# Hash-bucketed attention on one core: queries and keys turned in token order by VectorE, with contiguous casts, hashes and signs, and moves for two pairs at once

## The chip, the cores and the metric

The kernel runs on one core of one Trainium2 chip. The metric is the device time of one execution in microseconds; a kernel's time is the median of its runs. Besides these runs there is one profiled execution of each kernel, from which all rows below come.

## What is computed

Attention over 4 batches of 8 heads, 768 tokens of 64 dimensions each. A query sees only the keys with the same six hash bits. Its output goes through a mixture of eight low-rank adapters, of which each token uses the two with the largest gates.

```python
q_bits = (np.einsum('bhsd,dk->bhsk', q, proj) > 0)          # six bits per token
k_bits = (np.einsum('bhsd,dk->bhsk', k, proj) > 0)
mask   = q_bucket[:, :, :, None] == k_bucket[:, :, None, :]  # buckets: the bits as a number
scores = np.where(mask, q @ k.T / sqrt(64), -1e9)
attn   = softmax(scores)
x      = attn @ v                                            # as (3072, 512)
out    = x + sum over the two chosen e of w_e * (x @ A[e]) @ B[e]
```

## The kernel before, in words

**Pairs and tiles.** The 32 heads are worked on as 16 pairs of heads, p = 0 to 15; a batch has four pairs. For the first 14 pairs the scores of a pair are 9 tiles of 128 x 1024, stored keys by queries; the last two pairs are cut into groups of token blocks, so that the end can be worked off early. For each tile TensorE multiplies (`sc`), ScalarE takes the exponential into the buffer P (`ex`, L344), and TensorE multiplies with the values (`pv`, L366) into the one PSUM bank V, of which column 64 of each block is the softmax's sum. VectorE takes the reciprocal and multiplies (`rec`, `norm`), POOL casts the result (`xcast`), TensorE turns it (`xturn`), and per batch the adapters follow (`lzm`, `top`, `dif`, `sel`, `gexp`, `gate`, `zmul`, `delta`, `addx`, `store`).

**The mask as a part of the product.** The operands of the score matmul live in a tile aug: rows 0 to 63 are q or k of one head, transposed, and the rows from 64 on hold the hash bits as signs. For pairs 1 to 15 these are six rows and a constant one, 71 in all. Equal buckets add a constant to the score, and each differing bit takes enough away that the exponential is nothing. Where a query finds no key the softmax has to be uniform: for that, V begins with a tiny multiple (2 to the -56) of the sum of the values. POOL sums the values (`vsum`, L319 to L323), TensorE spreads the sum over the partitions (`uni`, L326, into the bank n), VectorE copies it out (`ucopy`, L330) and then into V ahead of each group (`seed`, L355 and L358).

**How a pair's aug is made.** Each partition holds six neighbouring tokens of a head (`l`, L272), so loads run over 1536 bytes. VectorE transposes 32 x 32 blocks of q or of k of both heads in one instruction of 768 elements (`t`, L278); in R the blocks lie by token within the partition, so the columns aren't in token order. POOL casts R to bf16 and puts the columns in order with the same instruction (`c`, L281): it writes 2-byte elements in steps of 12 bytes. SP then moves quarter-rows into aug, 8 DMAs a pair (`mv`, L286). Beside that TensorE hashes R in fp32 (`h`, L295), reading columns in steps of 256 bytes into n; VectorE turns the result into signs (`sn`, L299) and scales them (`sm2`, L303), and SP writes them to DRAM and back into the sign rows (`sdw`, `sdr`, L307 and L310). aug, P and R have four, three and two buffers.

**The first pair** is made faster: its tokens are transposed by TensorE, VectorE and ScalarE copy them out, POOL casts them into aug (`ca`, L250), TensorE hashes them (`ha`, L258), and VectorE writes 18 sign rows straight from PSUM (`sa`, L265), again in steps of 12 bytes; its aug has 82 rows.

**Order.** Each engine works its instructions in the order of a long string of such names (ORDER), written out by hand or by a planner; a name `mv.4.2.1` is the method with its arguments, mostly the pair first. SP's queue carries nearly all DMAs. An instruction that waits holds up all that stand behind it on its engine.

Of the kernel before, what the change touches and what calls it, by code (L numbers as in the profile page):

```python
# [75 lines left out]
class Kernel:  # L76

    def __init__(self, ctx, tc, q, k, v, proj, w_gate, A, Bm, out):
# [48 lines left out]
        self.ssc = t("ssc", [1])
        self.iq = t("iq", [4])
        self.thr = t("thr", [1])
        self.mul = t("mul", [1])  # L130
# [16 lines left out]
    def const2(self):  # L147
        nc = self.nc
        row = self.ident.rearrange("p (c r) -> p c r", c=4)
        iq, red = self.iq, nc.vector.tensor_reduce  # L150
        red(out=iq[:, 0:1], in_=row[:, 0:2, 12:18], axis=AX.XY, op=ALU.add)
        red(out=iq[:, 1:2], in_=row[:, 2:4, 6:12], axis=AX.XY, op=ALU.add)
        nc.vector.tensor_tensor(out=iq[:, 2:3], in0=iq[:, 0:1], in1=iq[:, 1:2], op=ALU.add)
        nc.vector.tensor_scalar(out=self.thr, in0=iq[:, 2:3], scalar1=-1.0, scalar2=None, op0=ALU.mult)
        nc.vector.tensor_scalar(out=self.mul, in0=iq[:, 2:3], scalar1=-48.0, scalar2=32.0,
                                op0=ALU.mult, op1=ALU.add)

    def const3(self):
        nc = self.nc
        row = self.ident.rearrange("p (j b i) -> p j b i", j=4, b=8)  # L160
        iq = self.iq
        nc.vector.memset(self.ssc, 32.0)
        for k, s in enumerate((-34.0, 3040.0)):
            nc.vector.tensor_reduce(out=iq[:, k:k + 1], in_=row[:, k::2, 6, :], axis=AX.XY, op=ALU.add)
# [536 lines left out]
```

## Time and profile before

| | |
|---|---|
| median of 3 runs | 240.85 us (237.78 to 241.51) |
| the profiled execution's own time | 237.42 us |
| its span | 235.6 us |
| mean granted clock of TensorE | 0.878 |
| busy: TensorE, VectorE, ScalarE, POOL | 184.8, 159.1, 147.6, 162.4 us |
| first exponential starts, last one ends | 17.98 us, 224.05 us |
| DMA: bytes, packets, share of the 16 engines (queue q1) | 32.67 MB, 41,021, 47.8% |

In the profile's rows a group is a line of the kernel on one engine: L281 is line 281, "POOL CAST Rb<-R 128x768" the engine, the operation, what it writes from what, and partitions x elements; after the count come busy time, the mean of one in ns, and the idle time of the engine just before, with what ended most of it. PE is TensorE's matmuls, PEld its weight loads, DVE is VectorE, ACT ScalarE, SPq the issuing of DMAs by SP. Matmuls are pipelined, so a busy PE isn't PE at its peak. The granted clock is the share of TensorE's clock that the throttle let through.

### The profile page before, as it was taken

What the parts mean: (1) busy time and instruction counts of PE and PEld (TensorE: products, weight loads), DVE (VectorE), ACT (ScalarE), POOL (GpSimd) and SP (SyncE); (2) the same over time, 40 slices, a digit from 0 to 9 for tenths busy, and PEclk for the clock granted to TensorE, in tenths of its full rate; (3) what the DMA queues carried; (4) which work ended last, traced back from release to release, by engine and by line L of the source; (5) the groups of instructions that cost most, each with busy time, mean ns of one, the idle gap of its engine ahead of it and who ended that gap; (6) DMA issues with size and microseconds to landing.
All of it is one profiled execution on the core that took longest, in us unless ns stands there. A gap on an engine that the chain in (4) does not pass through costs nothing.

```text
span 235.6 us, 5542 instructions
## 1 busy us (share of the span) xinstructions
PE 184.8 (78%) x2131; PEld 114.1 (48%) x2131; DVE 159.1 (68%) x364; ACT 147.6 (63%) x163; POOL 162.4 (69%) x168
## 2 busy tenths in 40 slices
PE   6566398598869999499867899979499965989652
PEld 2212143256346675275643556846255543877420
DVE  2799966369263479459857758986357963666894
ACT  2106188468755998377866868969467744799310
POOL 3899999996799698499757979892349990231000
PEclk9656589889985999679999999999769977899995
DMA  6911742684786661694366615564722322300445
GB/s 216 336 50 28 192 132 52 178 229 134 181 223 137 164 184 45 190 276 133 95 179 212 183 34 160 145 207 147 203 69 82 85 50 67 123 3 3 187 162 188
DMA packets 41495, 33.36 MB, mean 142 GB/s; under 512 B 25433, under 2 KB 38397, under 8 KB 41469
## 3 DMA queue, kind: packets, MB, share of 16 engines
q1 hardware_dynamic: 41021, 32.67, 47.8%
q8 instruction: 17, 0.28, 0.5%
q10 hardware_dynamic: 448, 0.33, 0.4%
q14 instruction: 9, 0.07, 0.1%
HBM read 20.06 MB, written 7.03 MB: 115 GB/s over the span
## 4 chain that ended last, share of the span: by engine, by line
PE 25%; POOL 24%; DVE 18%; DMA 9%; SPq 9%; issue 9%; ACT 4%; ACTq 0%; DVEq 0%; POOLq 0%
POOL Rb L281 17%; PE s L339 10%; SPq L286 7%; PE v L366 6%; DVE aug L265 6%; ACT P L344 4%; DMA aug<-Rb 4%; PE n L295 3%; DVE acc L490 3%; POOL va L319 3%; DMA proj<-in_proj_dram 2%; DMA vn<-in_v_dram 2%; DVE R L278 2%; DMA aug<-dr 2%; POOL vs L323 1%
## 5 line engine op out<-in xcount | busy, mean ns | idle before, releaser
L344 ACT ACTIVATE P<-s 128x1024 bf16<-128x1024 f32 (+1 forms) x146 | 142.9, 1045 | 64.2 <-PE s L339 62.1
L339 PE MATMUL s<-aug 71*128 71x256 bf16 (+4 forms) x432 | 101.5, 337 | 16.3 <-DMA aug<-Rb 9.1
L281 POOL CAST Rb<-R 128x768 bf16<-128x768 f32 x30 | 88.5, 3032 | 11.5 <-DMA aug<-Rb 10.4
L339 PEld LDWEIGHTS <-aug 71*128 71x128 bf16 (+1 forms) x432 | 45.3, 130 | 59.1 <-issue 36.7
L366 PEld LDWEIGHTS <-P 128*128 128x128 bf16 x1152 | 53.7, 103 | 22.1 <-issue 13.5
L366 PE MATMUL v<-vb,P 128*128 128x65 bf16 x1152 | 58.4, 200 | 3.4 <-DVE v L355 2.0
L295 PE MATMUL n<-R,hst 128*32 128x192 f32 x240 | 33.1, 610 | 1.9 <-POOL Rb L281 1.3
L278 DVE STREAM_TRANSPOSE R<-nat 128x768 f32<-128x768 f32 x30 | 29.8, 997 | 4.1 <-POOL Rb L281 3.9
L401 POOL CAST xb<-x 128x768 bf16<-128x768 f32 (+1 forms) x18 | 13.6, 756 | 27.3 <-DVE x L382 20.3
L319 POOL TENSOR_TENSOR va<-vn 128x384 f32<-128x384 f32 x16 | 17.7, 1116 | 6.2 <-DMA vn<-in_v_dram 6.1
L490 DVE SCALAR_TENSOR_TENSOR acc<-n,rt,x 128x512 f32<-128x512 f32 x17 | 12.7, 749 | 12.6 <-PE n L486 12.1
L382 DVE TENSOR_TENSOR x<-v,ri 128x384 f32<-128x384 f32 x28 | 16.8, 600 | 0.7
L299 DVE TENSOR_SCALAR sg<-n 128x192 bf16<-128x192 f32 x15 | 5.2, 349 | 17.4 <-PE n L295 17.4
L355 DVE COPY v<-u 128x390 f32<-128x390 f32 x28 | 15.8, 564 | 0.6
L314 POOL CAST vb<-vn 128x768 bf16<-128x768 f32 x16 | 13.5, 850 | 0.7 <-PE v L366 0.7
L413 DVE COPY xT<-n 128x768 bf16<-128x768 bf16 (+1 forms) x18 | 8.7, 484 | 7.1 <-PE n L408 6.8
L250 POOL CAST aug<-R 64x128 bf16<-64x128 f32 (+2 forms) x14 | 12.3, 1010 | 0.7 <-ACT R L243 0.5
L295 PEld LDWEIGHTS n<-R,hst 128*32 128x32 f32 x240 | 7.0, 120 | 11.8 <-issue 3.5
L303 DVE TENSOR_SCALAR s<-sg,ssc 128x192 bf16<-128x192 bf16 x15 | 12.5, 833 | 0.2
L372 DVE RECIPROCAL ri<-v 128x6 f32<-128x6 f32 x28 | 6.3, 225 | 9.0 <-PE v L366 8.6
L408 PE MATMUL n<-ident_bf,xb 128*128 128x128 bf16 x92 | 8.4, 225 | 2.5 <-DVE rt L466 2.3
L326 PE MATMUL n<-vs,eps 128*128 128x130 bf16 x16 | 3.8, 238 | 7.6 <-POOL vs L323 7.0
(83 smaller groups left out, 158.7 us busy)
## 6 DMA issues: line engine op xcount, KB each, us to landing
vn<-in_v_dram SPq DMA_DIRECT2D x16, 384.0 KB
nat<-in_k_dram SPq DMA_DIRECT2D x15, 384.0 KB
...
aug<-Rb SPq DMA_DIRECT2D x120, 48.0 KB
...
dr<-s SPq DMA_DIRECT2D x15, 48.0 KB
...
nat<-in_q_dram SPq DMA_DIRECT2D x2, 192.0 KB
```

The source lines that it names most:

```text
L265: self.nc.vector.tensor_scalar(out=self.augt(slice(64, 82), h, i, e, u, n), in0=self.hb(h)[r, u * P:(u + n) * P].rearrange("d (u p) -> d u ...
L278: self.nc.vector.transpose(out=self.R[p % 2][:, i], in_=self.nat[p % 3][:, i])
L281: self.nc.gpsimd.tensor_copy(out=self.Rb[p % 2][:, :, i].rearrange("p h f (c t) -> p h t f c", t=T), in_=self.R[p % 2][:, i].rearrange("p ...
L286: (self.nc.sync, self.nc.gpsimd)[eng].dma_start(out=self.aug[p % 4][32 * f:32 * f + 32, :, 192 * a:192 * a + 192], in_=self.Rb[p % 2][32 * ...
L295: self.nc.tensor.matmul(out=hs[32 * j:32 * j + 32], lhsT=self.hst[:, f].rearrange("p b i -> p (b i)"), rhs=rhs, start=(f == 0), stop=(f == ...
L319: add(out=a, in0=vn[:, :, 0:3, :], in1=vn[:, :, 3:6, :])
L339: self.nc.tensor.matmul(out=self.Sb[n % 3][:, o:o + qw], lhsT=aug[rows, 2 * h + 1, kt::T], rhs=aug[rows, 2 * h, q0:q0 + qw], start=True, s ...
L344: self.nc.scalar.activation(out=self.Pt[p % 3][:, at:at + w], in_=self.Sb[n % 3][:, 0:w], func=ACT.Exp, scale=0.125)
L355: self.nc.vector.tensor_copy(out=self.pvv(p, g), in_=self.u[p % 2][:, g:g + 1, :].to_broadcast([P, T, D + 1]))
L366: self.nc.tensor.matmul(out=v[:, i, :], lhsT=self.Pt[p % 3][:, o:o + P], rhs=self.vb[p % 3][:, h, kt, :], start=False, stop=(kt == T - 1), ...
L382: self.nc.vector.tensor_tensor(out=x[:, :, c:c + D], in0=v[:, :, 0:D], in1=self.ri[g % 2].unsqueeze(2).to_broadcast([P, T, D]), op=ALU.mult)
L490: self.nc.vector.scalar_tensor_tensor(out=self.acc[(m // 2) % 3][:, m % 2, lo:hi], in0=self.bank(bank)[:, lo:hi], scalar=self.rt[g % 2][:, ...
```

## The change

- **Transposes** (`t`): one instruction per head, 384 elements, reading q or k as before and writing R in token order, halves of the head dimension apart: the output steps 24 bytes from element to element.
- **Casts and hashes** (`c`, `h`): both now read R, and the cast writes Rb, in runs.
- **Signs**: the projection is negated once (`projx`). The signs are made by two bitwise operations on the upper half of each fp32 hash in PSUM (`bits`): sign bit kept, magnitude 16. That replaces compare, subtract and scale, the threshold and scale constants and the constant sign row; ScalarE's exponential gets a bias of -192 instead. All pairs have 70 rows.
- **Pair 0** is loaded so that its queries lie in token order, in runs of 256 bytes, and its casts and signs are written in runs.
- **Moves** (`mv`, `sdw`, `sdr`): for the pairs 2 and 3, 4 and 5 and so on at once, each of twice the size; aug has two buffers of two pairs each, in place of four of one. Pair 1 goes alone.
- **Uniform term** (`uv`): TensorE multiplies the sum of the values straight into V ahead of each group; `uni`, `ucopy` and `seed` are gone.
- **P** has two buffers in place of three. `dif`, `sel` and `gate` are written as scalar_tensor_tensor with a factor of 1.
- ORDER is new throughout.

```diff
-        self.dr = [dp.tile([P, 192], BF16, name=f"dr{i}") for i in range(2)]
+        self.dr = [dp.tile([2, P, 192], BF16, name=f"dr{i}") for i in range(2)]
...
-        self.Rb = r("Rb", 2, [2, 2, 2, 192], BF16)
-        self.sg = r("sg", 2, [192], BF16)
-        self.s2 = r("s2", 2, [192], BF16)
-        self.aug = r("aug", 4, [4, S], BF16)
+        self.Rb = r("Rb", 2, [2, 2, 2, 2, 192], BF16)
+        self.sg = r("sg", 2, [2, 192], U16)
+        self.aug = r("aug", 2, [8, S], BF16)
...
-        self.Pt = r("P", 3, [2 * T * S], BF16)
+        self.Pt = r("P", 2, [2 * T * S], BF16)
...
+        nc.vector.memset(self.bias, -192.0)
...
     def la(self, i, h, eng):
         (self.nc.sync, self.nc.scalar)[eng].dma_start(
-            out=self.natA[:, h, i], in_=self.qk[i][0, h].rearrange("(p t) d -> p (t d)", t=T))
+            out=self.natA[:, h, i].rearrange("p (t d) -> p t d", t=T),
+            in_=self.qk[i][0, h].rearrange(("(t p) d -> p t d", "(p t) d -> p t d")[i], t=T))
...
     def augt(self, rows, h, i, e, u, n):
-        return self.aug[0][rows, 2 * h + i].rearrange("d (p u e) -> d e u p", e=2, u=3)[:, e, u:u + n]
+        return self.aug[0][rows, 2 * h + i].rearrange("d (u e p) -> d e u p", e=2, u=3)[:, e, u:u + n]
...
+    def bits(self, out, in_):
+        self.nc.vector.tensor_scalar(out=out, in0=in_, scalar1=0x8000, scalar2=0x4180, op0=ALU.bitwise_and,
+                                     op1=ALU.bitwise_or)
+
     def sa(self, h, i, e, u, n):
         c = 2 * i + e
...
+        hi = self.hb(h)[32 * c:32 * c + 6, u * P:(u + n) * P].bitcast(U16).rearrange("d (u p w) -> d u p w", u=n, w=2)
+        self.bits(self.augt(slice(64, 70), h, i, e, u, n).bitcast(U16), hi[:, :, :, 1])
...
     def t(self, p, i):
-        self.nc.vector.transpose(out=self.R[p % 2][:, i], in_=self.nat[p % 3][:, i])
+        for h in range(2):
+            self.nc.vector.transpose(out=self.R[p % 2][:, i, h].rearrange("p (f c t) -> p t f c", f=2, t=T),
+                                     in_=self.nat[p % 3][:, i, h].rearrange("p (t f c) -> p t f c", f=2, t=T))
 
     def c(self, p, i):
-        self.nc.gpsimd.tensor_copy(
-            out=self.Rb[p % 2][:, :, i].rearrange("p h f (c t) -> p h t f c", t=T),
-            in_=self.R[p % 2][:, i].rearrange("p h (t f c) -> p h t f c", f=2, c=32))
+        self.nc.gpsimd.tensor_copy(out=self.Rb[(p // 2) % 2][:, p % 2, :, i].rearrange("p h f x -> p h (f x)"),
+                                   in_=self.R[p % 2][:, i])
 
     def mv(self, p, a, f, eng=0):
+        lo = 1 if p == 1 else 0
         (self.nc.sync, self.nc.gpsimd)[eng].dma_start(
-            out=self.aug[p % 4][32 * f:32 * f + 32, :, 192 * a:192 * a + 192],
-            in_=self.Rb[p % 2][32 * a:32 * a + 32].rearrange("d h i f x -> d (h i) f x")[:, :, f])
+            out=self.aug[(p // 2) % 2][32 * f:32 * f + 32, 4 * lo:8, 192 * a:192 * a + 192],
+            in_=self.Rb[(p // 2) % 2][32 * a:32 * a + 32, lo:2].rearrange("d j h i f x -> d (j h i) f x")[:, :, f])
 
     def h(self, p, f):
-        hs = self.Nb[:, 0:192].rearrange("m (c t) -> m c t", t=T)
         for j in range(4):
             h, i = divmod(j, 2)
-            rhs = self.R[p % 2][:, i, h, :].rearrange("p (t f c) -> p f c t", f=2, c=32)[:, f]
-            self.nc.tensor.matmul(out=hs[32 * j:32 * j + 32], lhsT=self.hst[:, f].rearrange("p b i -> p (b i)"),
-                                  rhs=rhs, start=(f == 0), stop=(f == 1), skip_group_check=True)
+            self.nc.tensor.matmul(out=self.Nb[32 * j:32 * j + 32, 0:192],
+                                  lhsT=self.hst[:, f].rearrange("p b i -> p (b i)"),
+                                  rhs=self.R[p % 2][:, i, h, 192 * f:192 * f + 192],
+                                  start=(f == 0), stop=(f == 1), skip_group_check=True)
...
     def sdr(self, p):
-        self.nc.sync.dma_start(out=self.aug[p % 4][64:71],
-                               in_=self.dr[p % 2].rearrange("(j b i) x -> b j (i x)", b=8, i=4)[0:7])
+        lo = 1 if p == 1 else 0
+        self.nc.sync.dma_start(out=self.aug[(p // 2) % 2][64:70, 4 * lo:8],
+                               in_=self.dr[(p // 2) % 2][lo:2].rearrange("q (j b i) x -> b (q j) (i x)", b=8, i=4)[0:6])
...
+    def uv(self, p, g):
+        if p < N - 2:
+            v = self.vs[p % 2][:, g:g + 1, :].to_broadcast([P, T, D + 1])
+        else:
+            v = self.vs[p % 2].unsqueeze(2).to_broadcast([P, 2, len(GROUPS[g]), D + 1])
+        self.nc.tensor.matmul(out=self.pvv(p, g), lhsT=self.eps, rhs=v, start=True, stop=False, skip_group_check=True)
...
-mv.4.0.0 sc.27.2 sc.27.1 h.5.0 l.7.1 seed.2.1 ex.27 vsum.4.0 sc.29.0 mv.4.1.0 sc.29.2 sc.29.1 sc.28.0 wload.5
+sc.30.2 mv.4.3.1 sc.30.1 pv.2.1.1.0 ex.29 sc.30.0 h.6.0 rec.2.1 norm.2.1 sc.31.0 sc.31.1 ex.30 xcast.2.0 sc.32.1
```

How the order moves, at three places. **VectorE at the start**, from the copies of pair 0's turned tokens to the signs of its second head; before:

```order
L243 COPY R_73<-s_66 128x128 x3
L265 TENSOR_SCALAR aug_81<-s_67,thr,mul 18x128 x2
L278 STREAM_TRANSPOSE R_74<-nat_71 128x768
L265 TENSOR_SCALAR aug_81<-s_67,thr,mul 18x128 x4
L278 STREAM_TRANSPOSE R_74<-nat_71 128x768
L265 TENSOR_SCALAR aug_81<-s_67,thr,mul 18x128 x2
L265 TENSOR_SCALAR aug_81<-s_67,thr,mul 18x2x128 x2
L265 TENSOR_SCALAR aug_81<-v,thr,mul 18x3x128
L299 TENSOR_SCALAR sg_78<-n 128x192
```

And now:

```order
L242 TENSOR_SCALAR aug_79<-s_67 6x128 x2
L222 COPY R_73<-s_66 128x128
L260 STREAM_TRANSPOSE R_74<-nat_71 128x6x64 x2
L242 TENSOR_SCALAR aug_79<-s_67 6x128
L260 STREAM_TRANSPOSE R_74<-nat_71 128x6x64 x2
L242 TENSOR_SCALAR aug_79<-s_67 6x128 x2
L242 TENSOR_SCALAR aug_79<-s_67 6x2x128
L242 TENSOR_SCALAR aug_79<-s_67 6x128 x3
L242 TENSOR_SCALAR aug_79<-s_67 6x2x128
L242 TENSOR_SCALAR sg_77<-n 128x192
L242 TENSOR_SCALAR aug_79<-v 6x3x128 x4
```

Pair 1's transposes, now four halves, still lie among the signs of pair 0, and its own signs come ahead of the four wide ones. **VectorE in the first pairs**, around the normalisations of pairs 0 and 1; before:

```order
L372 RECIPROCAL ri_130<-v 128x6
L382 TENSOR_TENSOR x_101<-v,ri_130 128x6x64
L355 COPY v<-u_97 128x390
L413 COPY xT_105<-n 128x768
L278 STREAM_TRANSPOSE R_74<-nat_72 128x768
L372 RECIPROCAL ri_131<-v 128x6
L382 TENSOR_TENSOR x_101<-v,ri_131 128x6x64
L330 COPY u_97<-n 128x130
L355 COPY v<-u_96 128x390
```

And now:

```order
L364 RECIPROCAL ri_125<-v 128x6
L374 TENSOR_TENSOR x_96<-v,ri_125 128x6x64
L260 STREAM_TRANSPOSE R_74<-nat_72 128x6x64 x2
L260 STREAM_TRANSPOSE R_73<-nat_71 128x6x64 x4
L364 RECIPROCAL ri_126<-v 128x6
L374 TENSOR_TENSOR x_96<-v,ri_126 128x6x64
```

The copies into V are gone, and up to six half transposes stand in a row ahead of a reciprocal. **SP's DMAs** for pairs 3 and 4 before, with the loads between:

```order
L307 DMA dr_60<-s_79 128x192
L286 DMA aug_84<-Rb_76 32x4x192
L272 DMA nat_71<-in_q_dram 128x2x384
L286 DMA aug_81<-Rb_75 32x4x192
L286 DMA aug_84<-Rb_76 32x4x192
L310 DMA aug_84<-dr_61 7x4x768
L286 DMA aug_81<-Rb_75 32x4x192
L286 DMA aug_84<-Rb_76 32x4x192
```

And now for pairs 2 and 3 together:

```order
L286 DMA dr_61<-sg_78 128x2x192
L269 DMA aug_80<-Rb_76 32x8x192 x6
L291 DMA aug_80<-dr_61 6x8x768
L269 DMA aug_80<-Rb_76 32x8x192 x2
```

Moves of two pairs, which alternated with loads between them, now stand as one batch.

More of the change, by code (lines that the diff above doesn't have):

```diff
@@ L14 @@
 BF16 = mybir.dt.bfloat16
+U16 = mybir.dt.uint16
 AX = mybir.AxisListType
@@ L123, in __init__ @@
         self.proj3 = t("proj3", [8])
-        self.px = t("px", [4, 32])
+        self.px = t("px", [2, 32])
         self.hst = t("hst", [2, 8, 4])
         self.eps = t("eps", [P], BF16)
[L127 to L130, printed above, removed]
+        self.bias = t("bias", [1])
         self.tiles = stream()
@@ L143, in const, with const5 @@
         nc.vector.memset(self.px, 0.0)
+        nc.vector.memset(self.bias, -192.0)
         make_identity(nc, self.ident)
         nc.scalar.activation(out=self.dume, in_=self.wz[:, 0:1], func=ACT.Exp)
[L147 to L164, printed above, removed]
-            nc.vector.scalar_tensor_tensor(out=self.ssc, in0=iq[:, k:k + 1], scalar=s, in1=self.ssc,
-                                           op0=ALU.mult, op1=ALU.add)
     def const4(self):
         nc = self.nc
+        nc.gpsimd.memset(self.hst, 0.0)
+    def const5(self):
+        nc = self.nc
+        nc.gpsimd.tensor_copy(out=self.ident_bf, in_=self.ident)
         nc.gpsimd.memset(self.eps, 2.0 ** -56)
-        nc.gpsimd.tensor_copy(out=self.ident_bf, in_=self.ident)
-        nc.gpsimd.memset(self.hst, 0.0)
         for a in self.vb:
@@ L336, in sc @@
         h, kt, q0, qw, o = segs[i]
-        rows = slice(0, 82 if p == 0 else 71)
-        aug = self.aug[p % 4]
-        self.nc.tensor.matmul(out=self.Sb[n % 3][:, o:o + qw], lhsT=aug[rows, 2 * h + 1, kt::T],
-                              rhs=aug[rows, 2 * h, q0:q0 + qw], start=True, stop=True)
+        aug = self.aug[(p // 2) % 2]
+        j = 4 * (p % 2) + 2 * h
+        if p:
+            lhsT = aug[0:70, j + 1, kt::T]
+        else:
+            lhsT = aug[0:70, j + 1, kt * P:kt * P + P]
+        rhs = aug[0:70, j, q0:q0 + qw]
+        self.nc.tensor.matmul(out=self.Sb[n % 3][:, o:o + qw], lhsT=lhsT, rhs=rhs, start=True, stop=True)
     def ex(self, n):
         p, at, w, segs = self.tiles[n]
-        self.nc.scalar.activation(out=self.Pt[p % 3][:, at:at + w], in_=self.Sb[n % 3][:, 0:w], func=ACT.Exp,
-                                  scale=0.125)
+        self.nc.scalar.activation(out=self.Pt[p % 2][:, at:at + w], in_=self.Sb[n % 3][:, 0:w], func=ACT.Exp,
+                                  scale=0.125, bias=self.bias)
     def pvv(self, p, g):
@@ L365, in pv @@
             o = p_col(p, h, kt, m)
-            self.nc.tensor.matmul(out=v[:, i, :], lhsT=self.Pt[p % 3][:, o:o + P], rhs=self.vb[p % 3][:, h, kt, :],
+            self.nc.tensor.matmul(out=v[:, i, :], lhsT=self.Pt[p % 2][:, o:o + P], rhs=self.vb[p % 3][:, h, kt, :],
                                   start=False, stop=(kt == T - 1), skip_group_check=True)
@@ L652 @@
+gexp.3.3 gate.3.3 addx.3.1.1.3 grec.3.2 zmul.3.3.0.1.0 store.3.1.0 addx.3.2.0.2 zturn.3.3.5 zout.3.3.5 norm.15.3.0
+store.3.2.0.0 delta.3.3.0.1 gsum.3.3 grec.3.3 addx.3.3.0.1.0.256 addx.3.3.0.1.256.512 store.3.2.0.1.0.256
+store.3.2.1.1.256.512
 """
```

313 lines of the change are left out of this document (148 added, 165 removed).

## The prediction

> **What bounds the kernel now.** I read the page first: the busy line and the chain of work that ended last.
>
> ```profile
> PE 184.8 (78%) x2131; PEld 114.1 (48%) x2131; DVE 159.1 (68%) x364; ACT 147.6 (63%) x163; POOL 162.4 (69%) x168
> POOL Rb L281 17%; PE s L339 10%; SPq L286 7%; PE v L366 6%; DVE aug L265 6%; ACT P L344 4%; DMA aug<-Rb 4%; PE n L295 3%; DVE acc L490 3%; POOL va L319 3%; DMA proj<-in_proj_dram 2%; DMA vn<-in_v_dram 2%; DVE R L278 2%; DMA aug<-dr 2%; POOL vs L323 1%
> ```
>
> No engine is full, and the chain jumps from POOL to SP, DMA, PE and DVE. So the kernel is held by waits between engines, and the bound changes with the place. Next the groups by line and the table of waits.
>
> ```profile
> L344 ACT ACTIVATE P<-s 128x1024 bf16<-128x1024 f32 (+1 forms) x146 | 142.9, 1045 | 64.2 <-PE s L339 62.1 <-PE v L366 1.5
> L281 POOL CAST Rb<-R 128x768 bf16<-128x768 f32 x30 | 88.5, 3032 | 11.5 <-DMA aug<-Rb 10.4 <-DVE gw L457 0.5 <-DVE s L303 0.3
> ...
> PE n L326 <- POOL vs L323: 7.0, 4, 2.6
> PE s L339 <- DMA aug<-Rb: 9.1, 4, 3.3
> PE s L339 <- DMA aug<-dr: 4.2, 2, 3.0
> PE v L194 <- DVE aug L265: 5.3, 1, 5.3
> PE v L366 <- DVE v L355: 2.0, 3, 1.1
> ```
>
> The 146 exponentials take 142.9 us and sit idle 62.1 us for scores. TensorE is late because its operands are: 9.1 + 4.2 us for moved rows and signs, 7.0 us for POOL's sums of V, 5.3 us for the signs of pair 0. POOL's cast of 3.03 us, 30 times, feeds all of that. Two stretches of 5 us (columns: PE, PEld, DVE, ACT, POOL busy, granted clock, DMA share, GB/s) show good running and the price of a stall, and two rows of ScalarE's timeline the ends of the dense part.
>
> ```profile
> 70.00:75.00 5.00, 5.00 (x55) 3.58 (x56) 2.34 (x5) 3.00 (x4) 5.00 (x3) 0.50 0.58 179
> 145.00:150.00 5.00, 4.86 (x71) 3.65 (x70) 4.56 (x10) 5.00 (x7) 4.69 (x5) 1.00 0.68 182
> ...
> 17.98 1.06 ACT L344 ACTIVATE P<-s 128x1024 bf16<-128x1024 f32 x1 [5.76 <-PE s L339]
> 223.03 1.02 ACT L344 ACTIVATE P<-s 128x1024 bf16<-128x1024 f32 x1 [1.47 <-PE v L366]
> ```
>
> At a granted clock of 1.00 TensorE (4.86 of 5) and ScalarE (5.00) are both full. Right after a stall of TensorE, at 70 to 75 us, the clock is 0.50 and ScalarE loses 2.0 us more. From 17.98 to 224.05 us ScalarE has some 143 us of work and takes 206; the 18.0 us before and the 11.5 us after (235.6 - 224.05) are start and tail.
>
> **Part 1, the start.** VectorE writes the signs of pair 0 with steps of 12 bytes; the change writes them in a run, and drops the casts' stride on POOL too.
>
> ```profile
> L265 DVE TENSOR_SCALAR aug<-v,thr,mul 18x384 bf16<-18x384 f32 x4 | 6.2, 1558 | 0.1
> L265 DVE TENSOR_SCALAR aug<-s,thr,mul 18x128 bf16<-18x128 f32 x8 | 6.0, 756 | 0.9 <-PE s L258 0.8
> L265 DVE TENSOR_SCALAR aug<-s,thr,mul 18x256 bf16<-18x256 f32 x2 | 2.5, 1236 | 0.0
> L299 DVE TENSOR_SCALAR sg<-n 128x192 bf16<-128x192 f32 x15 | 5.2, 349 | 17.4 <-PE n L295 17.4
> L278 DVE STREAM_TRANSPOSE R<-nat 128x768 f32<-128x768 f32 x30 | 29.8, 997 | 4.1 <-POOL Rb L281 3.9
> ```
>
> A strided 2-byte write costs 1558 / 384 = 4.06 ns per element; L299, read from PSUM and written in a run, 349 / 192 = 1.8, start included. The 14 sign instructions stay, by L299's row roughly 8 x 0.26 + 2 x 0.41 + 4 x 0.55 = 5.1 us instead of 14.7: 9.6 off VectorE. Two transposes of pair 1 sit among them and become four halves (part 5), some 2.2 us more. Net 7.4; I take **-7 us** of the path (first exponential some 4 us earlier, the 5.3 us stall gone, less a q load of 256-byte runs). Bounds: -9, and -3 if the loads set the start.
>
> **Part 2, the hash.** TensorE's hash now reads R in a run, not in steps of 256 bytes. Timeline rows, both at full clock:
>
> ```profile
> 7.01 0.42 PE L258 MATMUL s<-R,px 128*32 128x128 f32 x8 [1.14 <-DVE R L243]
> 63.78 1.10 PE L295 MATMUL n<-R,hst 128*32 128x192 f32 x8
> ```
>
> Contiguous, 8 x 128 columns take 0.42 us, 0.41 ns per column; strided, 8 x 192 take 1.10, 0.72 ns. So a group of eight falls to about 0.63 us. Of 30 groups 28 lie past the start: 28 x 0.47 = 13 us of TensorE time, which counts where TensorE is the limit: **-11 us** (0 if hidden, -13 if all counts).
>
> **Part 3, the uniform term.** One matmul of 130 columns, a copy out and a copy into V become one matmul of up to 390 columns straight into V.
>
> ```profile
> L355 DVE COPY v<-u 128x390 f32<-128x390 f32 x28 | 15.8, 564 | 0.6
> L330 DVE COPY u<-n 128x130 f32<-128x130 f32 x16 | 4.6, 285 | 4.9 <-PE n L326 4.7
> L326 PE MATMUL n<-vs,eps 128*128 128x130 bf16 x16 | 3.8, 238 | 7.6 <-POOL vs L323 7.0 <-DVE sg L299 0.7
> L486 PE MATMUL n<-Bcat,zT 128*128 128x512 bf16 x17 | 7.4, 438 | 0.7 <-DVE acc L490 0.3 <-DVE zT L483 0.2
> ```
>
> TensorE gets 28 of 390 columns, between 0.24 and 0.44 us by the two rows, 0.37, and 8 smaller of some 0.27: 12.5 us against 3.8, at most +8.7; overlapped with their neighbours +5. VectorE loses 20.4 us. The new matmul still waits for the normalisation that reads V, with the scores behind it in TensorE's queue, but 0.56 us less. The 7.0 us wait for POOL's sums mostly goes, since POOL is no longer behind. Sum +7 - 1.5 - 6 = about **-1 us**; bounds +9 and -5.
>
> **Part 4, cast and moves.** The cast becomes contiguous; the nearest row is the cast of V.
>
> ```profile
> L314 POOL CAST vb<-vn 128x768 bf16<-128x768 f32 x16 | 13.5, 850 | 0.7 <-PE v L366 0.7
> L286 SPq DMA_DIRECT2D aug<-Rb x120: 585/592/1588, 20.0 to 200.3; - x120
> 118.67 2.29 DMA aug<-Rb
> 131.97 3.67 DMA aug<-dr
> ```
>
> 30 x 0.85 = 25.5 us replaces 88.5: POOL falls from 162 to about 99 us. SP's move issues fall from 120 to 64 (8 for pair 1 alone, 8 for each of seven couples): 56 x 0.59 = 33 us of SP, if one of twice the size issues as fast. The bytes stay. On each queue the issues of one couple stand 4 to 6 score tiles ahead of their first use, about 4.4 to 6.6 us at 1.1 us a tile, against landings of 2.3 to 3.7 us. The stalls of TensorE, 13.3 us, come at about half as many boundaries; what a stall costs behind it, 2.0 us at half clock, goes with it. I take two thirds of 13.3 + 5 x 2.0 (five such stalls): **-16 us**, between -6 and -22. Late next are TensorE's own work and VectorE.
>
> **Part 5, the transposes.** 30 of 997 ns become 60 of half the size that write in steps of 24 bytes. No row shows a strided 4-byte write. Below: half of 997, 0.50 us; above: L265's 1.56 us for 384 strided 2-byte elements. In the middle, as a whole word is half of the strided case's trouble: 1.04 us each, 62 us in all, +33. VectorE then has 159.1 - 12.5 (the scaling of signs) - 20.4 - 9.6 + 33 = 150 us, still under the span, so most is hidden by TensorE; what shows is that runs of two, four, once six transposes (2.1, 4.2, 6.2 us) hold up a normalisation queued behind them, and with it TensorE's uniform matmul. **+4 us**, between 0 and +31 (half of the 64 that the upper row adds). The Trainium skill, "Vector Engine (DVE) Microarchitecture Reference", section "5.2 Measured stream behaviour on trn2", speaks against this step: a destination alone that steps 24 words costs about 2.5 ns a column, an estimate of 0.96 us for 384; no run here shows it, and the sum by it would be the same.
>
> **Part 6, gates and signs.** Tiny VectorE instructions take long while POOL works.
>
> ```profile
> L303 DVE TENSOR_SCALAR s<-sg,ssc 128x192 bf16<-128x192 bf16 x15 | 12.5, 833 | 0.2
> L457 DVE TENSOR_TENSOR gw<-m,e 128x24 f32<-128x24 f32 x6 | 7.5, 1247 | 0.2 <-ACT e L453 0.2
> L457 DVE TENSOR_TENSOR gw<-m,e 128x8 f32<-128x8 f32 x2 | 0.3, 154 | 0.0
> 110.20 1.90 DVE L457 TENSOR_TENSOR gw<-m,e 128x24 f32<-128x24 f32 x1
> 109.64 2.87 POOL L281 CAST Rb<-R 128x768 bf16<-128x768 f32 x1
> ```
>
> 24 elements took 1.90 us while the cast ran, and 154 ns for 8 in the tail with POOL idle. The scaling (12.5 us) is gone, and shorter casts shorten the rest whatever the new form does. Some of it delays ScalarE's gate exponential: **-3 us** (0 to -6). The two buffers of P instead of three cost nothing: a pair's exponentials begin some six tiles after the last values matmul that reads the buffer; without that, one tile, 1 us a pair. The bias operand replaces a sign row at no cost: ScalarE's instruction keeps its size.
>
> **Sum.** -7 - 11 - 1 - 16 + 4 - 3 = -34: a span of 235.6 - 34 = 201.6. The profiled run took 237.42, 1.8 more than its span, so 203.4; the median shown, 240.85, is 1.4% above that run: **206 us**.
>
> **Rivals.** (A) The couples starve, and it gets slower. Signs of two pairs now leave only after the second pair's hash. If order leaves no lead, each of seven boundaries pays signs out and back: 0.59 + 2.3 + 0.59 + 3.7, 7.2 us, and 2.0 at half clock, 64 us in place of 13.3. Sum -34 + 16 + 51 = +33, about 274 us. It decides from 5.2 us a boundary (2% slower). For it: today's landings do stall TensorE by up to 3.3 us. Against: the lead of 4 to 6 tiles, and POOL, which made moves late, has time. (B) VectorE becomes the bound: at 1.56 us a transpose, a run of four holds the queue 6.2 us, and half of 64 us shows: 201.6 - 4 + 32 = 229.6, about 235 us. For it: the 4.06 ns row; against: half-words there, whole words here. (C) The change doesn't do what it says on TensorE: the hash stays as dear, and the uniform term costs its +9: -34 + 11 + 10 = -13, 222.6, about 228 us. Against: the 0.42 us row.
>
> **Numbers.** Forecast 0.64, A 0.08, B 0.13, C 0.15. The range 189 to 230 reaches from the forecast with the moves at -22, the transposes free and some 7 us less stalling, up to C, and leaves out A and most of B. A measurement here tells about 2% from no change (236.0 and 245.7). Faster: the forecast, C and 0.06 of B, 0.85; same 0.05, slower 0.10 (A and 0.02 of B).
>
> **What would show it.** Right: casts near 0.85 us, POOL under 100 us; hash groups of eight near 0.6 us; first exponential near 14 us; no TensorE wait above 3 us on moved rows; ScalarE idle for scores near 30 us. Wrong: transposes above 1.3 us each with normalisation late behind them (B), TensorE waits of 5 us and more before pairs 2, 4, 6 and so on (A), hash groups still at 1.0 us (C).

## The result and the profile after

| | before | after |
|---|---|---|
| median of 3 runs | 240.85 us | 195.24 us (193.53 to 195.49) |
| ratio, 95% interval | | 0.815 [0.802, 0.828] |
| the profiled execution: own time, span | 237.42, 235.6 us | 193.53, 191.6 us |
| mean granted clock of TensorE | 0.878 | 0.933 |
| first exponential starts, last one ends | 17.98, 224.05 us | 18.94, 180.5 us |

A second measurement of the changed kernel, made with some of the experiments, gave 190.99 us and a ratio of 0.801 [0.796, 0.806]. In the two profiles, whose spans are 191.6 and 188.7 us, the difference arises early: by 44 us the second has done 19 exponentials, the first 16, and from 20 to 44 us its granted clock is 0.72 against 0.57. The kernel is faster by some 46 us; the forecast was 35. First the page's busy line and the chain that ended last, of the kernel after.

```profile
PE 168.7 (88%) x2143; PEld 114.2 (60%) x2150; DVE 120.6 (63%) x316; ACT 151.5 (79%) x163; POOL 93.7 (49%) x168
PE s L325 20%; ACT P L329 15%; PE v L358 10%; PE n L276 5%; DVE R L260 5%; DVE acc L484 3%; SPq L269 3%; DMA nat<-in_k_dram 3%; DMA wst<-in_moe_w_gate_dram 2%; DMA aug<-Rb 2%; PE v L351 2%; PE n L419 2%; DMA dr<-sg 1%; PE s L217 1%; PE n L400 1%
```

POOL's cast, 17% of the chain before, is gone from this list; two casts of 0.8 us are left in the chain. At the head stand TensorE's scores and values and ScalarE's exponentials: the work itself, not what feeds it. The groups that the prediction priced, in the same columns as before:

```profile
L329 ACT ACTIVATE P<-s,bias 128x1024 bf16<-128x1024 f32 (+1 forms) x146 | 147.5, 1172 | 17.1 <-PE s L325 16.0
L260 DVE STREAM_TRANSPOSE R<-nat 128x384 f32<-128x384 f32 x60 | 45.8, 862 | 2.1 <-DMA nat<-in_k_dram 1.3
L264 POOL CAST Rb<-R 128x768 bf16<-128x768 f32 x30 | 24.4, 825 | 20.9 <-DVE R L260 17.1
L276 PE MATMUL n<-R,hst 128*32 128x192 f32 x240 | 18.8, 375 | 0.8 <-DVE R L260 0.7
L351 PE MATMUL v<-vs,eps 128*128 128x390 bf16 (+2 forms) x36 | 11.7, 325 | 0.8 <-DVE x L383 0.7
```

The exponentials' idle time for scores fell from 62.1 to 16.0 us, further than the 30 of the prediction. The table of waits of TensorE alone, from its top:

```profile
PE s L217 <- DMA nat<-in_k_dram: 3.5, 1, 3.5
PE s L325 <- ACT P L329: 1.7, 4, 0.9
PE s L325 <- DMA wst<-in_moe_w_gate_dram: 1.5, 1, 1.5
```

No wait on moved rows or signs is left near the top; what leads is one load at the start. Where the time went is plain from the same stretches of both kernels (columns as in the prediction). Before:

```profile
20.00:44.00 24.00, 16.18 (x145) 7.76 (x144) 18.02 (x23) 14.58 (x14) 23.51 (x18) 0.83 0.46 131
44.00:94.00 50.00, 43.80 (x537) 27.05 (x537) 30.46 (x61) 36.80 (x38) 43.42 (x39) 0.90 0.62 158
94.00:175.00 81.00, 66.77 (x800) 43.32 (x797) 55.71 (x119) 57.59 (x63) 58.35 (x54) 0.92 0.56 161
```

After:

```profile
20.00:44.00 24.00, 22.01 (x166) 10.78 (x166) 13.51 (x23) 15.91 (x17) 15.13 (x22) 0.57 0.64 180
44.00:94.00 50.00, 47.89 (x688) 33.73 (x687) 34.23 (x78) 48.07 (x50) 28.75 (x44) 1.00 0.84 224
94.00:175.00 81.00, 78.22 (x1149) 59.69 (x1152) 51.67 (x135) 80.61 (x85) 39.96 (x65) 1.00 0.46 130
```

From 44 us on ScalarE is busy 48.07 + 80.61 of 131 us (before 36.80 + 57.59) at a granted clock of 1.00. Up to 44 us almost nothing was won, and the clock there is lower than before, 0.57. ScalarE's timeline of the kernel after says the same:

```profile
18.94 5.14 ACT L329 ACTIVATE P<-s,bias 128x1024 bf16<-128x1024 f32 x5 [3.93 <-PE s L325]
...
39.11 4.13 ACT L329 ACTIVATE P<-s,bias 128x1024 bf16<-128x1024 f32 x4 [1.16 <-PE s L325]
43.99 20.33 ACT L329 ACTIVATE P<-s,bias 128x1024 bf16<-128x1024 f32 x20 [0.75 <-PE s L325]
...
86.43 26.50 ACT L329 ACTIVATE P<-s,bias 128x1024 bf16<-128x1024 f32 x26
```

By 43.2 us 16 exponentials are done, before it was 15. Of the 130 that follow, most run without a gap and end at 180.5 us, 1.05 us apiece; before, 131 took from 43.2 to 224.05, 1.38 apiece. The whole gain lies in that stretch.

### The profile page after: what moved, and what is told of

Same layout as the page of the kernel before. It is cut to its first block, busy times and chain, and to the rows that moved or that the text cites. A ratio compares the mean times of both kernels' runs of the same rounds, so it can differ in the third digit from the quotient of the medians.

```text
span 191.6 us, 5425 instructions
## 1 busy us (share of the span) xinstructions
PE 168.7 (88%) x2143; PEld 114.2 (60%) x2150; DVE 120.6 (63%) x316; ACT 151.5 (79%) x163; POOL 93.7 (49%) x168
## 4 chain that ended last, share of the span: by engine, by line
PE 43%; ACT 16%; DVE 14%; issue 10%; DMA 9%; SPq 4%; POOL 2%; ACTq 1%; DVEq 0%; POOLq 0%
PE s L325 20%; ACT P L329 15%; PE v L358 10%; PE n L276 5%; DVE R L260 5%; DVE acc L484 3%; SPq L269 3%; DMA nat<-in_k_dram 3%; DMA wst<-in_moe_w_gate_dram 2%; DMA aug<-Rb 2%; PE v L351 2%; PE n L419 2%; DMA dr<-sg 1%; PE s L217 1%; PE n L400 1%
## 5 line engine op out<-in xcount | busy, mean ns | idle before, releaser
L329 ACT ACTIVATE P<-s,bias 128x1024 bf16<-128x1024 f32 (+1 forms) x146 | 147.5, 1172 | 17.1 <-PE s L325 16.0
L325 PE MATMUL s<-aug 70*128 70x256 bf16 (+2 forms) x432 | 103.3, 325 | 5.9 <-ACT P L329 1.7
L325 PEld LDWEIGHTS <-aug 70*128 70x128 bf16 x432 | 45.3, 127 | 23.3 <-issue 15.1
L260 DVE STREAM_TRANSPOSE R<-nat 128x384 f32<-128x384 f32 x60 | 45.8, 862 | 2.1 <-DMA nat<-in_k_dram 1.3
L264 POOL CAST Rb<-R 128x768 bf16<-128x768 f32 x30 | 24.4, 825 | 20.9 <-DVE R L260 17.1
L276 PE MATMUL n<-R,hst 128*32 128x192 f32 x240 | 18.8, 375 | 0.8 <-DVE R L260 0.7
L351 PE MATMUL v<-vs,eps 128*128 128x390 bf16 (+2 forms) x36 | 11.7, 325 | 0.8 <-DVE x L383 0.7
L463 POOL TENSOR_TENSOR zm<-lz,gw 128x128 bf16<-128x128 f32 x18 | 7.0, 401 | 10.0 <-DVE gw L451 10.0
L419 PEld LDWEIGHTS <-xT 128*128 128x128 bf16 x96 | 7.2, 98 | 2.1 <-issue 0.8
L304 POOL TENSOR_TENSOR vs<-vc,va 128x128 bf16<-128x128 f32 x16 | 7.3, 458 | 2.3 <-PE v L351 1.9
```

Source lines behind the costliest of these rows:

```text
L260: self.nc.vector.transpose(out=self.R[p % 2][:, i, h].rearrange("p (f c t) -> p t f c", f=2, t=T), in_=self.nat[p % 3][:, i, h].rearrange( ...
L264: self.nc.gpsimd.tensor_copy(out=self.Rb[(p // 2) % 2][:, p % 2, :, i].rearrange("p h f x -> p h (f x)"), in_=self.R[p % 2][:, i])
L276: self.nc.tensor.matmul(out=self.Nb[32 * j:32 * j + 32, 0:192], lhsT=self.hst[:, f].rearrange("p b i -> p (b i)"), rhs=self.R[p % 2][:, i, ...
L325: self.nc.tensor.matmul(out=self.Sb[n % 3][:, o:o + qw], lhsT=lhsT, rhs=rhs, start=True, stop=True)
L329: self.nc.scalar.activation(out=self.Pt[p % 2][:, at:at + w], in_=self.Sb[n % 3][:, 0:w], func=ACT.Exp, scale=0.125, bias=self.bias)
L351: self.nc.tensor.matmul(out=self.pvv(p, g), lhsT=self.eps, rhs=v, start=True, stop=False, skip_group_check=True)
```

## Experiments

The kernels were measured in three groups, each beside runs of the kernel before, whose median was 236.9, 237.8 or 239.3 us; so I compare ratios to it, and turn a difference of ratios into us with that median. The change itself stands at 0.801 to 0.815; "above the change" gives the difference to both.

### The token order: transposes, casts and hash

Three kernels undo parts of it in the changed kernel. The first puts the old block form of `t`, `c` and `h` back.

```diff
-        for h in range(2):
-            self.nc.vector.transpose(out=self.R[p % 2][:, i, h].rearrange("p (f c t) -> p t f c", f=2, t=T), ...
+        self.nc.vector.transpose(out=self.R[p % 2][:, i], in_=self.nat[p % 3][:, i])
```

> The changed kernel with the turn in token order undone: one transpose of 768 elements into blocks, POOL puts the columns in order with 2-byte writes in steps of 12 bytes, the hash reads in steps of 256 bytes; all else, the new order included, is kept. Theory (the runs of elements in cast and hash carry the gain): POOL is back at about 160 us busy in a new order that counts on short casts, the hash costs TensorE 14 us more, and ScalarE no longer runs without gaps: 225 us or more. Rival (the new order, the couples and the uniform term carry it): 205 us or less.

Measured: 223.98 us, 0.947 [0.938, 0.955], 31 to 34 us above the change; the theory, to within a microsecond of its bound. The rival, that the block form costs little, fell. The second undoes the hash's reads alone.

```diff
-                                  rhs=self.R[p % 2][:, i, h, 192 * f:192 * f + 192],
+            rhs = self.R[p % 2][:, i, h, :].rearrange("p (t f c) -> p f c t", f=2, c=32)[:, f]
```

> The changed kernel, but the hash reads R in steps of 256 bytes as before, which takes the columns in a wrong order, so the masks are not the reference's; casts and transposes as changed. Theory (TensorE is close behind ScalarE, so its 14 us count): groups of eight back at 1.0 to 1.1 us, 201 to 207 us. Rival (TensorE's time is hidden behind ScalarE, which is the bound now): 198 us or less.

Measured: 200.83 us, 0.848 [0.840, 0.857], 8 to 11 us above the change; by the time just below the theory's range. The start blurs this: from 20 to 44 us the granted clock was 0.93 here and 0.57 and 0.72 in the two profiles of the change, and by 44 us this kernel has done 20 exponentials against 16 and 19. Counted from there, at 1.05 us for each exponential of the lead, its last exponential ends some 10.5 us later than in either of them, an estimate. The third undoes the casts' writes alone.

```diff
-        self.nc.gpsimd.tensor_copy(out=self.Rb[...].rearrange("p h f x -> p h (f x)"), in_=self.R[p % 2][:, i])
+        self.nc.gpsimd.tensor_copy(out=self.Rb[...].rearrange("p h f (c t) -> p h t f c", t=T),
+                                   in_=self.R[p % 2][:, i].rearrange("p h (t f c) -> p h t f c", f=2, c=32))
```

> The changed kernel, but POOL writes the cast in steps of 12 bytes as before, which leaves aug's columns in a wrong order, so scores belong to the wrong tokens; transposes and hash as changed. Theory (POOL's casts set when moves start): 3.0 us a cast, POOL busy about 158 us, moves late again, 212 to 225 us. Rival (POOL at 158 of 195 us still has room and the couples' lead covers it): 200 us or less. Beside it the gate product of 24 elements: near 0.2 us if the new form of the instruction is what made it short, above 0.8 us if the short casts did.

Measured: 220.42 us, 0.926 [0.913, 0.939], 26 to 30 us above the change; the theory by the time. Three of its waits, and VectorE's groups with shapes kept apart, which answer to part 6 of the prediction:

```profile
ACT P L330 <- PE s L326: 37.3, 24, 6.2
...
PE n L401 <- POOL xb L394: 6.6, 4, 3.0
PE s L326 <- DMA aug<-Rb: 4.6, 1, 4.6
```

```profile
L442 DVE SCALAR_TENSOR_TENSOR m<-lz,top 128x24 f32<-128x24 f32 x6 | 5.7, 946 | 0.1
L436 DVE SCALAR_TENSOR_TENSOR d<-lz,top 128x24 f32<-128x24 f32 x6 | 3.0, 502 | 0.0
L452 DVE SCALAR_TENSOR_TENSOR gw<-m,e 128x24 f32<-128x24 f32 x6 | 1.1, 182 | 2.2 <-ACT e L448 2.2
```

The same three groups with short casts, in the kernel after:

```profile
L435 DVE SCALAR_TENSOR_TENSOR d<-lz,top 128x24 f32<-128x24 f32 x6 | 1.5, 250 | 0.0
L451 DVE SCALAR_TENSOR_TENSOR gw<-m,e 128x24 f32<-128x24 f32 x6 | 1.2, 205 | 3.7 <-ACT e L447 3.7
L441 DVE SCALAR_TENSOR_TENSOR m<-lz,top 128x24 f32<-128x24 f32 x6 | 1.2, 197 | 0.1
```

ScalarE's idle time for scores is back at 37.3 us from the casts alone. The theory's way was that moves come late. TensorE does wait for moved rows again, 4.6 us, but longer, 6.6 us, for POOL's cast of a normalised result (`xcast`): the longest of these waits, 3.0 us, ends at 95.03 us, behind two long casts in a row on POOL (88.98 to 94.34 us) and the short cast that follows them.

Of the gates, the expectation had named the product gw. It stayed short, 182 ns, which by that test would speak for the new form of the instruction. But none of its six ran beside a long cast, while d and m, in the new form too, are held now and then (502 and 946 ns against 250 and 197): a d of 1.88 us at 89.47 us and an m of 1.89 us at 92.03 us lie within those two casts, and an m of 2.43 us at 145.88 us beside four shorter POOL instructions in a row. So it is POOL's work that holds them, not the old form. Last, the token order by itself in the kernel before, whose order, moves, signs and uniform term stay.

```diff
-        self.nc.vector.transpose(out=self.R[p % 2][:, i], in_=self.nat[p % 3][:, i])
+        for h in range(2):
+            self.nc.vector.transpose(out=self.R[p % 2][:, i, h].rearrange("p (f c t) -> p t f c", f=2, t=T), ...
...
+        self.nc.gpsimd.tensor_copy(out=self.Rb[p % 2][:, :, i].rearrange("p h f x -> p h (f x)"), in_=self.R[p % 2][:, i])
...
+                                  rhs=self.R[p % 2][:, i, h, 192 * f:192 * f + 192],
```

> The kernel before, its order, moves, signs and uniform term untouched, with only the transposes, casts and hash in token order (t, c and h). Theory: short casts and hashes are worth most of their gain in the old order too, POOL's busy time falls from 162 to about 100 us and the hash by 13 us: 0.88 to 0.94 of the time before. Rival: the old order was fitted to long casts and the stalls move elsewhere (copies into V, the bank n, and 46 us or less of VectorE that the slower transposes add): 0.97 or more.

Measured: 215.17 us, 0.908 [0.896, 0.920], a gain of 22 us; the theory. The gates' instructions, in the old form here, are short as well with the short casts: 334, 259 and 240 ns for d, m and gw, before 656, 522 and 1247. So the token order alone brings half of the whole gain, but taking it away from the change costs 31 to 34 us. The same edit has two prices, by what stands around it.

### The uniform term

The changed kernel with the old term: TensorE into n, VectorE out of n, VectorE into V, so for all pairs and groups in the order.

```diff
-vsum.0.2 sc.3.0 t.3.0 l.4.0 sc.3.2 h.2.0 vcast.1 ex.3 sdr.1 sc.5.1 uv.0.0 sc.5.2
+vsum.0.2 uni.0 ucopy.0 sc.3.0 t.3.0 l.4.0 sc.3.2 h.2.0 vcast.1 ex.3 sdr.1 sc.5.1 seed.0.0 sc.5.2
```

> The changed kernel with the uniform term as before: a matmul of 130 columns, a copy out and a copy into V by VectorE ahead of each group, put where the bank is free; all else as changed. Theory (a wash: TensorE gets 8 us back, VectorE 20 us more, neither is the bound): within 3 us of the changed kernel, 193 to 199 us. Rival (the copies sat between the groups of values on the path): 201 us or more.

Measured: 218.45 us, 0.911 [0.899, 0.924], 23 to 26 us above the change. "A wash" fell and the rival was right. Two kernels split this. One begins V by VectorE's copy alone, from a constant tile, with no matmul.

```diff
-        self.nc.tensor.matmul(out=self.pvv(p, g), lhsT=self.eps, rhs=v, start=True, stop=False, ...)
+        self.nc.vector.tensor_copy(out=self.pvv(p, g), in_=v)
```

> The changed kernel, but V is begun by a VectorE copy from a constant tile ahead of each group, with no matmul and no waiting for sums: it leaves the true uniform term out and puts only the copy of 0.56 us back between a normalisation and the next group's values. Theory A (the copy lies in the ring values, reciprocal, normalisation, copy, values through the one bank V, and each turn is longer by it): most of the 23 us by which the full undoing was slower, 208 to 215 us. Theory B (the 130-column matmul and its copy out, which share bank n with hashes and turns, made that loss): within 4 us of the changed kernel, 192 to 199 us.

Measured: 202.41 us, 0.849 [0.843, 0.855], 11.4 us above the change in the same group. It fell between the theories. TensorE's longest wait in it:

```profile
PE v L360 <- DVE v L353: 15.0, 24, 1.5
```

The other keeps the matmul into V and puts the detour through the bank n back as work that nothing reads, once a pair.

```diff
-vsum.0.2 sc.3.0 t.3.0 l.4.0 sc.3.2 h.2.0 vcast.1 ex.3 sdr.1 sc.5.1 uv.0.0 sc.5.2
+vsum.0.2 uni.0 ucopy.0 sc.3.0 t.3.0 l.4.0 sc.3.2 h.2.0 vcast.1 ex.3 sdr.1 sc.5.1 uv.0.0 sc.5.2
```

> The change with the old detour through the bank n put back as extra work, 16 times: TensorE multiplies the sum of the values into n (about 0.24 us each), VectorE copies it out (about 0.29 us each), and nothing reads the copy; V still begins by TensorE alone. Theory: the bank n is the other half of what the old uniform term cost, since the matmul waits for POOL's sums with the scores behind it and hash, turned x and adapters share n: 0.84 to 0.87 of the time before, some 9 to 15 us above the change. Rival: the extra work is 16 x 0.24 us of TensorE and 16 x 0.29 us of VectorE and not more, and the other half lies in something else: at most 0.825, under 5 us above the change.

Measured: 198.37 us, 0.829 of the time before. Its four runs lie between 194.2 and 202.7 us, too far apart for an interval; by the medians it is 3 to 7 us above the change. The theory of 9 to 15 us fell. So the copy that stands between one group's normalisation and the next group's values costs 11 us, the bank some 5 (roughly, as its runs scatter), and with both there 23 to 26 are lost. The remaining 5 to 11 us appear only when the two stand in one chain. What makes them is open: in the full undoing TensorE waits 17.1 us for the copies into V, little more than the 15.0 with the copy alone, and VectorE 11.9 us for the matmul into n, against 9.9 with the detour alone; the granted clock is lower too, 0.867 against 0.895 and 0.953.

### The couples

The changed kernel, its moves and sign DMAs split per pair, still issued at the couple's place in the order.

```diff
-        dma_start(out=self.aug[...][32 * f:32 * f + 32, 4 * lo:8, ...], in_=self.Rb[...][32 * a:32 * a + 32, lo:2] ...)
+        for j in range(lo, 2):
+            dma_start(out=self.aug[...][32 * f:32 * f + 32, 4 * j:4 * j + 4, ...], in_=self.Rb[...][32 * a:32 * a + 32, j] ...)
```

> The change with the moves and the signs' DMAs issued per pair instead of per couple, one right after the other: the same bytes, but 56 more moves of the old size and 14 more sign DMAs, some 40 us more of issuing on SP's queue (0.59 us each). Theory: SP has the room, so the couples' half number of issues is worth little: 0 to 4 us above the change, at most 0.825 of the time before. Rival: fewer issues are what took the stalls on moved rows away: 8 us or more above the change, 0.845 or above, with TensorE waiting for moved rows again.

Measured: 219.17 us, 0.926 [0.914, 0.938], 27 to 30 us above the change; the rival. TensorE's waits in it:

```profile
PE s L327 <- DMA aug<-Rb: 12.3, 4, 5.8
...
PE s L327 <- DMA aug<-dr: 2.7, 1, 2.7
```

And SP's issues in the kernel after and then in this one (minimum, median and longest in ns, first and last start):

```profile
L269 SPq DMA_DIRECT2D aug<-Rb x64: 585/599/2376, 17.2 to 153.1; - x64
```

```profile
L270 SPq DMA_DIRECT2D aug<-Rb x120: 585/599/2152, 17.7 to 177.5; - x120
```

An issue takes 0.6 us whether it moves 48 or 96 KB, so twice the issues cost SP twice the time, and the waits on moved rows return: 12.3 and 2.7 us, where the change has none. The longest of these waits, on SP's timeline and then TensorE's:

```profile
64.72 1.23 SPq L270 DMA_DIRECT2D aug<-Rb  x2
66.05 0.83 SPq L293 DMA_DIRECT2D aug<-dr  x2
66.93 1.23 SPq L270 DMA_DIRECT2D aug<-Rb  x2
...
70.41 0.39 PE L327 MATMUL s<-aug 70*128 70x256 bf16 x1 [5.81 <-DMA aug<-Rb]
```

SP issues almost without a gap here, from 57.4 to 73.6 us; the last moves before the wait ends are issued from 66.93 to 68.16 us, while TensorE stands idle, and it starts 2.3 us after that. The page's busy line doesn't list SP at all, and yet its 0.6 us an issue decide here when a couple's last row lands. The waits in the table sum to 15.0 us; the granted clock fell as well, from 0.933 to 0.857, and no run parts that from the rest of the 27 to 30 us.

### The transposes

The changed kernel with each transpose made twice.

```diff
-        for h in range(2):
+        for h in (0, 0, 1, 1):
```

> The change with each transpose of 384 elements made twice, the second the same as the first: 60 more of 0.76 to 0.86 us, some 46 to 52 us more of VectorE, which then is busy about 167 us. Theory: VectorE has that room and only runs of transposes that stand ahead of a normalisation show: 1 to 8 us above the change, 0.80 to 0.84 of the time before. Rival (the one in which VectorE becomes the bound, as a dear transpose would have made it): half of the added time or more shows, 0.90 or above.

Measured: 246.09 us, 1.032 [1.017, 1.047], 52 to 55 us above the change and slower than the kernel before. The theory of room on VectorE fell altogether. The page's busy line, its chain and its group of transposes:

```profile
PE 192.6 (78%) x2143; PEld 126.1 (51%) x2150; DVE 171.7 (70%) x376; ACT 155.1 (63%) x163; POOL 93.9 (38%) x168
...
DVE R L260 33%; PE s L325 18%; PE v L358 10%; PE n L276 4%; DVE acc L484 3%; ACT P L329 2%; PE n L419 2%; DMA nat<-in_k_dram 2%; PE v L351 2%; DVE xT L405 1%; PE n L400 1%; PE s L217 1%; DVE x L374 1%; PE n L480 1%; DVE aug L242 1%
...
L260 DVE STREAM_TRANSPOSE R<-nat 128x384 f32<-128x384 f32 x120 | 97.3, 860 | 2.9 <-POOL Rb L264 0.6
```

97.3 - 45.8 = 51.5 us were added to VectorE, and the whole amount shows, though VectorE is busy only 70% of the span. TensorE's two longest waits:

```profile
PE n L276 <- DVE R L260: 9.5, 6, 3.3
PE v L351 <- DVE x L374: 5.7, 3, 3.8
```

It waits most for the transposes themselves, in the hash that reads R, and then for the normalisation that must have read V. A piece of VectorE's timeline tells how the second comes about:

```profile
67.05 3.37 DVE L260 STREAM_TRANSPOSE R<-nat 128x384 f32<-128x384 f32 x4
70.28 0.15 DVE L364 RECIPROCAL ri<-v 128x6 f32<-128x6 f32 x1
70.48 0.56 DVE L374 TENSOR_TENSOR x<-v,ri 128x384 f32<-128x384 f32 x1
70.95 0.35 DVE L242 TENSOR_SCALAR sg<-n 128x192 uint16<-128x192 uint16 x1
71.22 6.54 DVE L260 STREAM_TRANSPOSE R<-nat 128x384 f32<-128x384 f32 x8
77.62 0.15 DVE L364 RECIPROCAL ri<-v 128x6 f32<-128x6 f32 x1
77.82 0.56 DVE L374 TENSOR_TENSOR x<-v,ri 128x384 f32<-128x384 f32 x1
```

In this piece the reciprocals follow the runs of transposes without a gap and wait for nothing else: they are late because of the run ahead of them. TensorE's next matmul into V and, behind it in the queue, its scores wait in turn. A part of the loss is TensorE's own: the same 2143 matmuls are busy 192.6 us here and 168.7 in the kernel after, at a granted clock of 0.831 against 0.933.

### The start and the bias

In the kernel before, pair 0's k was loaded ahead of the projection on ScalarE's queue; the change loads it behind. This puts it ahead again.

```diff
-la.0.0.0 lproj la.1.0.1 const
+la.0.0.0 la.1.0.1 lproj const
```

> The changed kernel with the first k load issued ahead of the two loads of the projection, as before the change, and nothing else moved. Theory (the order of issue on ScalarE's queue made k land at 7.4 us instead of 4.4): the first exponential 2 to 3 us earlier than 18.9 us and the time 1.5 to 3 us shorter. Rival (the q loads in runs of 256 bytes keep the DMA engines full, and k lands late whatever its place): first exponential within 0.7 us of 18.9, time unchanged within 1 us.

Measured: 187.97 us, 0.788 [0.782, 0.794], against 0.801 [0.796, 0.806] for the change in the same group: 3.0 us less, the theory, and the fastest kernel of this study. TensorE's first turns in the kernel before, in the kernel after, then in this one, and this one's first exponentials:

```profile
4.45 0.63 PE L238 MATMUL s<-ident,nat 128*128 128x128 f32 x4 [0.52 <-DMA nat<-in_k_dram]
```

```profile
7.45 0.66 PE L217 MATMUL s<-ident,nat 128*128 128x128 f32 x2 [3.52 <-DMA nat<-in_k_dram]
```

```profile
3.90 0.35 PE L217 MATMUL s<-ident,nat 128*128 128x128 f32 x1
```

```profile
15.43 4.13 ACT L329 ACTIVATE P<-s,bias 128x1024 bf16<-128x1024 f32 x4 [3.92 <-PE s L325]
```

The last kernel does without the bias operand, with smaller signs; keys of other buckets are then not masked.

```diff
-... scalar1=0x8000, scalar2=0x4180, ...        scale=0.125, bias=self.bias)
+... scalar1=0x8000, scalar2=0x4000, ...        scale=0.125)
```

> The changed kernel with no bias in the exponential and signs of size 2 in place of 16, so that numbers stay finite; keys of other buckets are then not masked. Theory (the bias operand lengthens the exponential): busy time per exponential back from 1.01 to 0.98 us, and since ScalarE runs without gaps for some 130 us, 3 to 5 us shorter. Rival (the longer rows come from running back to back, or from the place of P, not from the bias): 1.01 us as it was and the time within 1 us.

Measured: 191.50 us, 0.795 [0.785, 0.805]: no difference from the change that can be told. The exponentials (minimum, median, longest in ns) in the second measurement of the change, and then without the operand:

```profile
L329 ACT ACTIVATE P<-s,bias x146: 687/1132/1382, 18.1 to 176.0; 128x1024 bf16<-128x1024 f32 x142, 128x512 bf16<-128x512 f32 x4
```

```profile
L329 ACT ACTIVATE P<-s x146: 597/1024/1102, 18.1 to 176.5; 128x1024 bf16<-128x1024 f32 x142, 128x512 bf16<-128x512 f32 x4
```

And their groups on the two pages, in the same order:

```profile
L329 ACT ACTIVATE P<-s,bias 128x1024 bf16<-128x1024 f32 (+1 forms) x146 | 147.6, 1151 | 14.6 <-PE s L325 13.6
```

```profile
L329 ACT ACTIVATE P<-s 128x1024 bf16<-128x1024 f32 (+1 forms) x146 | 137.5, 1019 | 23.8 <-PE s L325 21.9 <-PE n L419 0.9
```

The operand makes each exponential 0.1 us longer, 10 us in all (busy time of the groups), but without it the idle time for scores grows from 13.6 to 21.9 us. The start has a share in that: from 32 to 44 us the granted clock was 0.50 here and 0.93 in the measurement beside it, and by 44 us three exponentials fewer are done. From 44 to 170 us, both granted 1.00, it does 125 exponentials against 123, so past the start the operand costs some 2 us of the 10, an estimate from these two profiles that the medians are too coarse to confirm. TensorE stands right behind ScalarE; neither alone is the bound now.

## Why the prediction was right, and where it was not

**The direction and the mechanism held.** The forecast was that POOL's long casts and the strided hash make TensorE's operands late, and that with them gone the waits go. The casts' price came out as priced (825 ns for 850), POOL at 93.7 us (under 100), the hash at 18.8 / 30 = 0.63 us a group (0.63), and no wait on moved rows above 3 us. Undoing the casts, the uniform term or the couples brought ScalarE's idle time for scores back (37.3, 33.8 and 39.0 us). Rivals A and C fell: no couple starved, the hash became cheap, and the uniform term, whose matmuls did take 7.9 us more of TensorE (11.7 for 3.8), won far more than that.

**Part 1, the start (-7 us, first exponential near 14 us), failed.** The signs became as short as expected (14 in some 5.3 us by their rows) and the 5.3 us stall went, but the first exponential started at 18.94 us, a microsecond later than before. The step that failed is that the loads would not set the start: I priced a q load of short runs and passed over the k load, which the change had moved behind the projection. TensorE's first turn waited for it until 7.45 us, against 4.45 us before. Moved back, the first exponential starts at 15.43 us, 1.4 us from the forecast. From TensorE's first turn to the first exponential it is 11.5 us in the changed kernel with either order, before 13.5: the shorter signs and casts won 2 us there, not the 4 that the prediction put on the first exponential.

**Part 2, the hash (-11 us), held**: undone alone, 8 to 11 us, and some 10.5 once the different starts are taken out.

**Part 3, the uniform term (-1 us, bounds +9 and -5), was far too small.** Undone it costs 23 to 26 us, outside both bounds. The sum entered the new matmuls with +7 us, where the line above it says +5 overlapped; that is a slip, but a small one. The step that failed is the wait: I took off 28 times 0.56 us at a tenth of their worth, because the table before showed only 2.0 us of TensorE waiting for the copy into V. That table names what came last. In the kernel with the copy alone, where casts and moves are short, the copy comes last 24 times, 15.0 us. That those other waits covered it before is the likely reading; no run takes them away in the kernel before with the copy kept.

**Part 4, cast and moves (-16 us, -6 to -22), had the right cause and too small a size.** Undoing the casts costs 26 to 30 us, undoing the couples 27 to 30. Two paths were missing from it. It priced the long casts by the waits on moved rows alone, 13.3 us, while in the kernel with long casts TensorE waits longer for the cast of the results behind them on POOL (6.6 us) than for moved rows (4.6). And it counted the 33 us of SP's issues but let them weigh nothing of their own; the split kernel shows that they decide when the last row of a couple lands.

**Part 5, the transposes (+4 us, 0 to +31), had a price inside its bounds and a wrong cover.** One took 862 ns, not 1.04 us. (The Trainium skill, "Vector Engine (DVE) Microarchitecture Reference", section "5.2 Measured stream behaviour on trn2", gives about 2.5 ns a column for a destination alone that steps 24 words, from which the prediction's estimate of 0.96 us came. This kernel steps 24 bytes, six words, so that row is only near the case; the measurement, 2.24 ns an element, decides.) But the step "VectorE then has 150 us, still under the span, so most is hidden" is refuted: VectorE was busy only 120.6 us, not 150, and yet 51.5 us more on it cost 52 to 55. What is queued behind VectorE's long instructions, and who waits for them, sets the price, not its share. Rival B was therefore nearer than its 0.13: at that slope a transpose of 1.56 us, 60 x 0.70 = 42 us more, would have brought the kernel back to some 237 us, an estimate from this one slope. And the 0.18 us by which each came out shorter than I took are 11 us by the same slope, as much as the forecast was too high; that this is the reason is not shown, since other terms missed on both sides.

**Part 6.** The gates' instructions shortened as expected (gw from 1247 to 205 ns), by the short casts and not by the new form. That this won the 3 us was not measured by itself. "The bias operand at no cost" was right in time as far as the medians can tell, and wrong in its reason: the instruction does get longer. The Trainium skill, "ScalarE: Activation LUTs", section "What ACT_TABLE_LOAD costs", gives 93 ns for such an operand; the trace agrees, with 108 ns between the medians. Most of the price is covered, some 2 us may not be, because TensorE is almost as full as ScalarE.

**The sum.** The span came out at 191.6 instead of 201.6 us. The first exponential came 5 us later than forecast, and the stretch from it to the last one's end took 161.6 us where 201.6 - 14 - 11.5 = 176.1 were forecast. The single undoings add up to 81 to 90 us (31 to 34, 23 to 26, 27 to 30), twice what the change won: each part, left undone, would alone have held the kernel near 220 us. What the new order is worth by itself was not measured. These prices contain the lower granted clock of the kernels with new waits as well (0.86 to 0.91, against 0.933). A sum of parts priced one at a time in the old order could not see that; that it landed near is in part luck, since its errors lay on both sides.
